# One attention and expert kernel: the last pair's sums, copies and divisions in another order, and the last batch's token bookkeeping made inside the first expert tile

## The chip, the cores and the metric

The kernel runs on one core of one Trainium2 chip. The metric is the time of one execution in microseconds (us) on the device; "before" is the kernel as it stood, "after" the changed one. A core has five engines that run their own instruction streams side by side and wait for each other by semaphores: PE (TensorE, matrix products), DVE (VectorE), ACT (ScalarE), POOL (GpSimd) and SP (SyncE, here only an issuer of transfers). ACT, SP and POOL each issue DMA transfers, which 16 DMA engines then carry out. PE's clock has two levels, 1.2 and 2.4 GHz; the profile lists what was granted in a stretch as a share of the upper one, so 0.50 is the lower level and 1.00 the upper.

## What is computed

Attention for 4 batches and 12 heads over 448 positions with heads of width 64, with a tanh cap on the scores. Its result, laid out as 1792 tokens of width 768, goes through a layer of 8 experts: each token goes to the one expert whose normalised embedding is nearest to it, and is scaled by a gate.

```python
scores = q @ k.T / sqrt(64)
scores = cap * np.tanh(scores / cap)
attn = softmax(scores)
x = (attn @ v)                      # as 1792 tokens x 768
logits = (x / |x|) @ (emb / |emb|).T / tau
expert = argmax(logits)             # one of 8
gate = softmax(logits)[expert]
out[expert == e] = gate * (relu(x @ w1[e]) @ w2[e])   # w1: 768x1024, w2: 1024x768
```

## The kernel before, in words

**Attention.** The 48 heads are worked as 24 pairs, six for each batch. The loop `for i in range(NPAIRS + 1)` in `attention_bounded` runs, in each pass, the scores of pair i (`scores`, four pieces u = 0 to 3) and the values of pair i-1 (`values`, also four pieces); the probabilities go to SBUF as `prob`. The sums over the keys that the softmax is divided by are not taken by a reduction but by adding blocks of `prob` (`add_keys`: one DVE addition at L792, two or three more at L798 and L800 on POOL, for the last pair half of them on DVE) and then multiplying by ones on PE (`norms`, tile `d`, L837, copied to `ds` by DVE at L839). `norms_t` transposes `ds` and takes reciprocals (`inv`). `rows` transposes the unnormalised output `xt` of a pair back to tokens (tile `xb`, L861) and divides it on DVE into `xsb` (L866). `router` and `router_t` make the experts' logits (`lp`, `ls`, `lt`, `lgh` at L897).

The order on every engine inside this function is the order in which the code is written (`tc.manual_schedule`). Work that follows a pair is put into a list of steps (`after`, `later`), and `do_later` takes the next step at fixed points of the loop; `fill` is a second list, of halves of the first expert's weights that are split into two 16-bit parts (`split_first`, ACT L221 and DVE L222).

**The first expert.** The tokens of batches 0 to 2 are known before the last batch, so the expert with the most of them is started early. After the loop its first tile of 128 tokens is transposed (`transpose_x`, PE L212; ACT casts it to `xh`, DVE takes the rest `xl` at L216), then 12 blocks of 12 matmuls (`up`, tile `hp`, PE L231) make the hidden layer in two halves. Between the blocks the loop `while later or ups` places one step of the last two pairs each: `norms`, `norms_t`, `router`, `router_t`, `rows` twice, `write_rows`. Then `tile0` runs the 8 down products of this tile (`down`, tile `yp`, PE L638). Its `hooks` place other work ahead of a down product: hook 12 holds `choose` (the last batch's choice of expert, DVE L414 to L422) and `all_norms` (squares on ACT L384, a power on POOL L387), hook 15 `count_last` (`rank` and `counts` on PE L443 to L458, then some 20 small DVE rows from L473 to L590), hook 16 `scales_x` and `gates` (DVE L397 to L427). Near its end the next tile is transposed, and DVE's L668 and ACT's L669 scale the result.

**The second tile.** `tile_body(0, idx0[:, 1:2], ...)` stands behind the branch that chose the attention arm. Its hook 0 holds `order` (the order of the other experts: `perm`, `which_e`, `pos_e`, DVE L1174 to L1183), `start_loads` (SP reads `pos_e` into registers and issues ten transfers of the next expert's weights, `w1r` and `w2r`, 6 MB in all), `gates_out` (four DVE rows, then ACT writes two columns of 448 token rows to DRAM, L407 and L410: 8 bytes for each token), and `slots` (DVE: `every`, `gn`, `first_t`; the one-hot rows `a_all` at L484; about 16 small rows from `both` to `slot`; the wide comparison `bm` at L1216). Hook 8 holds `fill_table`: PE's `tabp` (L1227) needs `bm` and `a_all`; DVE turns it into `table` (L1228), POOL copies a column to `idx_in` (L197) and gathers 128 token rows `xg` from DRAM (L198), which become `x_tile` of the third tile (L204). This gather reads what the gates' write has put into DRAM, so it waits for that write too.

The third tile and those after it split the next expert's weights on ACT and DVE while PE works.

## Time and profile before

| | |
|---|---|
| median of 3 runs | 546.03 us (545.84, 546.03, 549.48) |
| the profiled execution, its own time | 543.88 us |
| its span, first to last instruction | 542.1 us |
| mean granted clock of PE over the span | 0.963 |
| busy share: PE, DVE, ACT, POOL | 89%, 61%, 55%, 45% |

The change touches a stretch from about 225 to 282 us of the span. The busy shares are means over all stages and tell little of it; the rows below are from that stretch. Times in them count from the start of the span.

### The profile page before, as it was taken

How to read it: one execution, taken by the hardware profiler on the slowest of the kernel's cores; microseconds unless marked ns; L12 is line 12 of the kernel's file. 1: busy time of each engine (PE TensorE's matmuls, PEld its weight loads, DVE VectorE, ACT ScalarE, POOL GpSimd, SP SyncE). 2: the span in 40 equal slices, each digit the busy share in tenths (PEclk: the TensorE clock that was granted, in tenths of full speed). 3: DMA queues.
4: the chain of work that ended last, by engine and by line, in shares of the span. 5: the costliest groups of instructions: out<-in, count | busy, mean ns of one | idle time of the engine just before them, and what ended most of it. 6: DMA issues, size and time to landing. Idle time of an engine off the chain costs nothing. (4 is left out here: it accounts for less than half of the span.)

```text
span 542.1 us, 11950 instructions
## 1 busy us (share of the span) xinstructions
PE 482.8 (89%) x4603; PEld 312.3 (58%) x4604; DVE 329.5 (61%) x712; ACT 300.5 (55%) x371; POOL 245.6 (45%) x294
## 2 busy tenths in 40 slices
PE   3999999999997979979698799999999999998970
PEld 1444444444443434347676578877887788777650
DVE  4876686868698679588719521771125812496710
ACT  3987789788978887926128210831115511567410
POOL 2567556564643454640136412843235623553531
PEclk9999999999999979989999799999999999998995
DMA  7433218331451540325299711491112931297921
GB/s 228 128 112 113 76 63 289 111 112 67 148 207 62 190 160 0 104 73 164 97 390 365 282 40 59 175 344 59 61 60 96 382 114 61 87 366 258 332 86 39
DMA packets 30595, 83.51 MB, mean 154 GB/s; under 512 B 7293, under 2 KB 7449, under 8 KB 30498
## 3 DMA queue, kind: packets, MB, share of 16 engines
q1 hardware_dynamic: 26354, 67.68, 35.7%
q0 software_dynamic: 2896, 13.00, 6.8%
q10 hardware_dynamic: 1248, 1.64, 0.9%
q8 instruction: 47, 0.77, 0.6%
q14 instruction: 50, 0.41, 0.2%
HBM read 69.91 MB, written 13.00 MB: 153 GB/s over the span
## 5 line engine op out<-in xcount | busy, mean ns | idle before, releaser
L780 ACT ACTIVATE prob<-s,icap 128x896 f32<-128x896 f32 x96 | 86.3, 904 | 24.7 <-PE s L774 16.7
L794 POOL TENSOR_TENSOR sums<-sums,prob 128x896 f32<-128x896 f32 x23 | 48.4, 2102 | 81.8 <-DVE sums L792 62.7
L231 PEld LDWEIGHTS <-h 128*128 128x128 f16 x1056 | 79.7, 99 | 7.4 <-issue 3.8
L784 ACT ACTIVATE prob<-prob,cap_b 128x896 f32<-128x896 f32 (+1 forms) x64 | 81.7, 1277 | 2.1
L231 PE MATMUL h<-xh,h 128*128 128x128 f16 (+1 forms) x480 | 78.7, 218 | 2.6 <-ACT x_tile L669 1.4
L231 PE MATMUL h<-xl,h 128*128 128x128 f16 (+1 forms) x480 | 78.8, 218 | 0.9 <-issue 0.9
L231 PE MATMUL h<-xh,l 128*128 128x128 f16 (+1 forms) x480 | 78.8, 218 | 0.5 <-issue 0.4
L811 PE MATMUL v<-prob,vb 128*64 128x448 f32 x288 | 72.2, 581 | 2.9 <-DVE xt L826 2.8
L800 POOL TENSOR_TENSOR sums<-sums,prob 64x448 f32<-64x448 f32 x47 | 64.6, 1375 | 3.6
L204 POOL TENSOR_TENSOR x_tile<-xg 128x768 f32<-128x768 f32 x17 | 25.3, 1489 | 83.8 <-PE xt L212 74.1
L231 PEld LDWEIGHTS <-l 128*128 128x128 f16 x528 | 51.8, 99 | 1.1 <-issue 1.1
L215 ACT CAST xh<-xt 128x384 f16<-128x384 f32 x32 | 13.9, 481 | 68.5 <-PE xt L212 60.5
L244 DVE SCALAR_TENSOR_TENSOR hl<-h,hh 128x512 f16<-128x512 f32 (+1 forms) x20 | 13.3, 664 | 62.6 <-ACT hh L243 62.6
L243 ACT ACTIVATE hh<-h 128x512 f16<-128x512 f32 (+1 forms) x20 | 11.5, 574 | 67.1 <-PE h L231 67.1
L774 PE MATMUL s<-hi 64*128 64x448 f32 x144 | 35.5, 484 | 14.1 <-DVE hi L756 11.8
L1388 PE MATMUL h<-xh,h 128*128 128x160 f16 x192 | 41.1, 237 | 5.1 <-ACTq L1526 2.6
L216 DVE TENSOR_TENSOR xl<-xt,xh 128x384 f16<-128x384 f32 x32 | 16.4, 551 | 46.3 <-ACT xh L215 46.2
L638 PEld LDWEIGHTS <-hh 128*128 128x128 f16 (+1 forms) x352 | 32.9, 100 | 19.4 <-issue 1.2
L222 DVE SCALAR_TENSOR_TENSOR l<-w1r,by_pos,h 128x1024 f16<-128x1024 f32 x30 | 37.7, 1305 | 9.8 <-ACT h L221 9.8
L774 PEld LDWEIGHTS s<-hi 64*128 64x128 f32 x144 | 14.4, 190 | 46.9 <-ACT prob L780 16.0
L1388 PE MATMUL h<-xh,l 128*128 128x160 f16 x192 | 41.1, 238 | 0.0
L1388 PE MATMUL h<-xl,h 128*128 128x160 f16 x192 | 41.0, 237 | 0.0
(312 smaller groups left out, 1132.0 us busy)
## 6 DMA issues: line engine op xcount, KB each, us to landing
w1r<-in_moe_w_dram SPq DMA_DIRECT2D x36, 512.0 KB, 6.8
w2r<-in_moe_w_dram SPq DMA_DIRECT2D x24, 768.0 KB, 7.2
qkb<-in_qk_pairs_dram SPq DMA_DIRECT2D x11, 960.0 KB, 5.1
vb<-in_v_pairs_dram SPq DMA_DIRECT2D x12, 512.0 KB, 5.7
x_dram<-xsb SPq DMA_DIRECT2D x4, 1152.0 KB, 6.5
ring<-in_moe_w_dram SPq DMA_DIRECT2D x6, 512.0 KB, 3.9
ring<-in_moe_w_dram SPq DMA_DIRECT2D x8, 384.0 KB, 3.2
x_dram<-xsb ACTq DMA_DIRECT2D x1, 1152.0 KB
```

The source lines that it names most:

```text
L204: nc.gpsimd.tensor_tensor(x_tile, xg[:, :D], xg[:, SCALE : SCALE + 1].to_broadcast([P, D]), op=ALU.mult)
L216: nc.vector.tensor_tensor(lo, t, hi, op=ALU.subtract)
L222: nc.vector.scalar_tensor_tensor(out=lo, in0=raw, scalar=scale, in1=hi, op0=ALU.mult, op1=ALU.subtract, accum_out=acc)
L231: nc.tensor.matmul(hp[:, f, :W], l[j][:, c], x[:, j, :W], start=j == 0 and f == 0 and n == 0, stop=j == DC - 1 and f == 3 and n == 2, skip ...
L638: nc.tensor.matmul(y, hidden[h][l][:, c, o : o + k], w2p[p % 2][w][f // 2][:, f % 2, m * C : (m + 1) * C], start=f == 0 and n == 0, stop=f ...
L774: nc.tensor.matmul(sp[:, s, :S], l[sl, kc], r[sl, :], start=n == 0, stop=n == 2)
L780: nc.scalar.activation(o, d, AF.Tanh, scale=icap)
L784: nc.scalar.activation(o, o, AF.Exp, scale=cap_b)
L794: nc.gpsimd.tensor_tensor(t, t, pt[:, 4:6, :], op=ALU.add)
L800: eng.tensor_tensor(t[sl, s, :], t[sl, s, :], pt[sl, 6, :], op=ALU.add)
L811: nc.tensor.matmul(o[s * DH : (s + 1) * DH, :S], vb[:, u, s * DH : (s + 1) * DH], pt[:, 2 * u + s, :], start=u == 0, stop=False, skip_grou ...
L1388: nc.tensor.matmul(o, w1p[p % 2][l][j][:, c], x[:, j, :], start=j == 0 and f == fs[0] and m == 0, stop=j == DC - 1 and f == fs[-1] and m == 2,
```

## The change

Three things are done.

1. **The last pair's sums, copies and divisions.** `add_keys` is cut into `add_two`, `add_third` and `add_left`. For pair 23 `add_two` is placed in the loop ahead of the copy of pair 22's output; of the other additions, those of the second head stay on POOL, and those of the first are put one by one on DVE between the divisions `xsb`. The copy of pair 23's output (`xt`) and the copies `ds` of pairs 22 and 23 move from DVE to ACT.
2. **The choice and the counts.** `do_later` takes no step before the first up block, so the transposed tile's first block stands ahead of `norms`. `choose(b)` is placed behind `router_t`, ahead of the two `rows`; `count_last` behind them, ahead of `write_rows`.
3. **The slots and the experts' order.** `slots` is cut into `slots_1`, `token_rows`, `slots_2` and `fill_masks`. In `tile0`, hook 12 now holds `all_norms`, hook 14 `slots_1`, hook 15 `scales_x` and `gates`, hook 16 `slots_2` and `order`. Hook 0 of the second tile keeps `start_loads`, `token_rows`, `fill_masks` and `gates_out`, in this order.

```diff
-        def tile0(todo, space):
+        def tile0(todo, space, counted=False):
...
-            hooks[12] += [lambda: choose(last), lambda: all_norms(last)]
-            hooks[15] += [count_last]
-            hooks[16] += [lambda: scales_x(last), lambda: gates(last)]
+            if counted:
+                hooks[12].insert(0, lambda: all_norms(last))
+                hooks[14] += [lambda: slots_1()]
+                hooks[15] += [lambda: scales_x(last), lambda: gates(last)]
+                hooks[16] += [lambda: slots_2(), order]
...
+            def add_two(i):
+                pt = prob[i]
+                t = sums[i] = apool.tile([P, 2, S], F32, tag="sums", name=f"sums{i}", bufs=3)
+                nc.vector.tensor_tensor(t, pt[:, 0:2, :], pt[:, 2:4, :], op=ALU.add)
+
+            def add_third(i, s, eng):
+                eng.tensor_tensor(sums[i][:, s, :], sums[i][:, s, :], prob[i][:, 4 + s, :], op=ALU.add)
+
+            def add_left(i, s, eng):
+                sl = slice(s * DH, (s + 1) * DH)
+                eng.tensor_tensor(sums[i][sl, s, :], sums[i][sl, s, :], prob[i][sl, 6, :], op=ALU.add)
+
             def add_keys(i):
-                pt = prob[i]
-                t = apool.tile([P, 2, S], F32, tag="sums", name=f"sums{i}", bufs=3)
-                nc.vector.tensor_tensor(t, pt[:, 0:2, :], pt[:, 2:4, :], op=ALU.add)
-                if i < NPAIRS - 1:
-                    nc.gpsimd.tensor_tensor(t, t, pt[:, 4:6, :], op=ALU.add)
+                if i == NPAIRS - 1:
+
+                    add_third(i, 1, nc.gpsimd)
+                    add_left(i, 1, nc.gpsimd)
+                    return
+                add_two(i)
+                nc.gpsimd.tensor_tensor(sums[i], sums[i], prob[i][:, 4:6, :], op=ALU.add)
                 for s in range(2):
...
-                    nc.vector.tensor_copy(x, o[:, :S])
+                    (nc.vector.tensor_copy if i < NPAIRS - 1 else nc.scalar.copy)(x, o[:, :S])
...
-                nc.vector.tensor_copy(ds, d[:, :S])
+                (nc.vector.tensor_copy if i < NPAIRS - 2 else nc.scalar.copy)(ds, d[:, :S])
...
+                if j == NPAIRS - 1:
+                    steps.insert(4, lambda: choose(b))
+                    steps += [nop, count_last]
...
+                        if i == NPAIRS and u < 2:
+                            (add_third, add_left)[u](j, 0, nc.vector)
...
+                        if (i, u) == (NPAIRS - 1, 2):
+                            add_two(i)
...
                 while later or ups:
-                    do_later()
+                    if len(ups) < 2 * DC:
+                        do_later()
...
     hooks1 = {
-        0: [order, start_loads, lambda: gates_out(last), slots],
+        0: [start_loads, lambda: token_rows(last), fill_masks, lambda: gates_out(last)],
```

Three places show how the instructions move. In the rows, `l` is the low part of a split weight, `ring` its raw piece, `hl` the low part of the hidden layer; numbers behind names tell buffers apart.

DVE around the last pair's sums, before:

```order
L826 COPY xt_2193<-v_2135 128x448
L897 TENSOR_TENSOR lgh<-lt_2195,inv_2000 128x3x64
L897 TENSOR_TENSOR lgh<-lt_2195,inv_2000 64x64
L222 SCALAR_TENSOR_TENSOR l_154,sums<-ring_178,first_s,h_150 128x384
L792 TENSOR_TENSOR sums_2205<-prob_2125 128x896
L798 TENSOR_TENSOR sums_2205<-sums_2205,prob_2125 128x448
L800 TENSOR_TENSOR sums_2205<-sums_2205,prob_2125 64x448
L866 TENSOR_TENSOR xsb<-xb_2214,inv_2000 128x3x128
```

And DVE at the same place after:

```order
L845 TENSOR_TENSOR sums_2190<-prob_2129 128x896
L888 COPY xt_2199<-v_2139 128x448
L959 TENSOR_TENSOR lgh<-lt_2201,inv_2004 128x3x64
L959 TENSOR_TENSOR lgh<-lt_2201,inv_2004 64x64
L222 SCALAR_TENSOR_TENSOR l_154,sums<-ring_178,first_s,h_150 128x384
L848 TENSOR_TENSOR sums_2190<-sums_2190,prob_2129 128x448
L928 TENSOR_TENSOR xsb<-xb_2217,inv_2004 128x3x128
L928 TENSOR_TENSOR xsb<-xb_2217,inv_2004 64x128
L222 SCALAR_TENSOR_TENSOR l_154,sums<-ring_179,first_s,h_150 128x384
L852 TENSOR_TENSOR sums_2190<-sums_2190,prob_2129 64x448
L928 TENSOR_TENSOR xsb<-xb_2229,inv_2004 128x3x128
```

Three additions in a row ahead of the first division have become one ahead of the copy, one ahead of the first division and one ahead of the second.

DVE between the last division and the last batch's choice, before:

```order
L866 TENSOR_TENSOR xsb<-xb_2365,inv_2000 128x3x128
L866 TENSOR_TENSOR xsb<-xb_2365,inv_2000 64x128
L244 SCALAR_TENSOR_TENSOR hl_210,acc_213<-hp_2257,hh_209 128x512
L222 SCALAR_TENSOR_TENSOR l_156,sums<-ring_180,first_s,h_152 128x384 x2
L222 SCALAR_TENSOR_TENSOR l_157,sums<-ring_178,first_s,h_153 128x384 x2
L222 SCALAR_TENSOR_TENSOR l_157,sums<-ring_179,first_s,h_153 128x384 x2
L244 SCALAR_TENSOR_TENSOR hl_212,acc_213<-hp_2258,hh_211 128x512
L414 TENSOR_REDUCE lg<-lgh 128x32
```

And DVE from the end of the choice to the counts, after:

```order
L420 TENSOR_REDUCE fm_2367<-first_2364 128x4
L422 TENSOR_TENSOR oh_all<-iota_v,fm_2367 128x32
L244 SCALAR_TENSOR_TENSOR hl_214,acc_217<-hp_2261,hh_213 128x512
L222 SCALAR_TENSOR_TENSOR l_156,sums<-ring_180,first_s,h_152 128x384
L928 TENSOR_TENSOR xsb<-xb_2386,inv_2004 128x3x128
L928 TENSOR_TENSOR xsb<-xb_2386,inv_2004 64x128
L222 SCALAR_TENSOR_TENSOR l_156,sums<-ring_180,first_s,h_152 128x384
L928 TENSOR_TENSOR xsb<-xb_2407,inv_2004 128x3x128
L928 TENSOR_TENSOR xsb<-xb_2407,inv_2004 64x128
L222 SCALAR_TENSOR_TENSOR l_157,sums<-ring_178,first_s,h_153 128x384 x2
L473 TENSOR_TENSOR own_2454<-rp_2442,oh_all 128x32
```

The choice now stands ahead of the two divisions `xsb`, and the counts (from L473) follow them behind two split steps. PE's rank product L443 takes the PSUM buffer that the first of these two divisions reads, and L457 the buffer of the second (there are two, `ps_t`).

DVE at the start of the second tile, before:

```order
L1174 TENSOR_TENSOR perm<-iota_t,place 128x64
L1181 TENSOR_TENSOR which_e<-perm,iota_t 1x64
L1183 TENSOR_REDUCE pos_e<-which_e 1x8
L432 TENSOR_REDUCE gs_4029<-ex 128x4
L433 TENSOR_SCALAR gs_4029<-gs_4029 128x4
L434 RECIPROCAL gs_4029<-gs_4029 128x4
L435 TENSOR_TENSOR xsb<-gs_4029,p2x 128x4
L1187 TENSOR_TENSOR every<-done_full,halves 128x8
```

And after:

```order
L484 TENSOR_SCALAR a_all<-iota_p,rowf,tok 128x128 x4
L1242 TENSOR_TENSOR bm<-iota_t,slot 128x640
L432 TENSOR_REDUCE gs_4095<-ex 128x4
L433 TENSOR_SCALAR gs_4095<-gs_4095 128x4
L434 RECIPROCAL gs_4095<-gs_4095 128x4
L435 TENSOR_TENSOR xsb<-gs_4095,p2x 128x4
```

The order of the experts has gone to the first tile, and the four rows of the gates, which ACT's write waits for, stand behind `a_all` and `bm` now.

## Rows read from the trace of the kernel before

**Rows 1.** Timeline of PE: start, duration, engine, line, what; in brackets the wait ahead.

```profile
234.20 0.52 PE L212 MATMUL xt<-ident,x_tile 128*128 128x128 f32 x3 [2.72 <-DVE xsb L866]
...
236.41 1.72 PE L837 MATMUL d<-sums,ones 128*32 128x448 f32 x8
238.07 0.29 PE L231 MATMUL hp<-xh,h 128*128 128x128 f16 x1
...
243.56 0.22 PE L231 MATMUL hp<-xh,h 128*128 128x128 f16 x1
...
244.23 0.50 PE L861 MATMUL xb<-ident,xt 128*128 128x128 f32 x3
...
249.36 0.49 PE L638 MATMUL yp<-h,hh 128*128 128x384 f16 x2
...
260.32 0.22 PE L231 MATMUL h<-xh,h 128*128 128x128 f16 x1 [1.38 <-ACT x_tile L669]
...
268.50 0.56 PE L1227 MATMUL tabp<-bm,a_all 128*128 128x40 f16 x16 [2.66 <-DVE bm L1216]
...
279.92 0.88 PE L212 MATMUL xt<-ident,x_tile 128*128 128x128 f32 x6 [0.38 <-POOL x_tile L204]
```

**Rows 2.** Windows: length, busy PE, PEld, DVE, ACT, POOL; PE clock; DMA share, GB/s.

```profile
236.00:239.00 3.00, 3.00 (x20) 1.22 (x19) 2.72 (x7) 1.50 (x3) 2.22 (x4) 0.50 0.43 131
...
269.80:273.20 3.40, 2.95 (x30) 2.76 (x28) 0.97 (x3) 0.00 (x0) 1.06 (x1) 0.50 0.94 331
```

**Rows 3.** Timeline of DVE, same columns.

```profile
228.43 2.02 DVE L792 TENSOR_TENSOR sums<-prob 128x896 f32<-128x896 f32 x1
...
243.28 0.60 DVE L222 SCALAR_TENSOR_TENSOR l<-ring,first_s,h 128x384 f16<-128x384 f32 x1
...
243.81 0.74 DVE L866 TENSOR_TENSOR xsb<-xb,inv 128x384 f32<-128x384 f32 x2
...
250.98 0.85 DVE L414 TENSOR_REDUCE lg<-lgh 128x32 f32<-128x384 f32 x1
...
253.40 0.19 DVE L473 TENSOR_TENSOR own<-rp,oh_all 128x32 f32<-128x32 f32 x1 [0.46 <-PE cp L458]
...
256.04 0.16 DVE L397 COPY p2x<-den 128x4 f32<-128x4 f32 x1
...
257.87 1.02 DVE L216 TENSOR_TENSOR xl<-xt,xh 128x384 f16<-128x384 f32 x2 [0.66 <-ACT xh L215]
...
261.88 0.23 DVE L1174 TENSOR_TENSOR perm<-iota_t,place 128x64 f32<-128x64 f32 x1 [2.22 <-issue]
...
263.80 0.97 DVE L484 TENSOR_SCALAR a_all<-iota_p,rowf,tok 128x128 f16<-128x128 f16 x4
264.69 0.16 DVE L1196 SCALAR_TENSOR_TENSOR both<-done_full,tails 128x8 f32<-128x8 f32 x1
...
267.62 0.82 DVE L1216 TENSOR_TENSOR bm<-iota_t,slot 128x640 f16<-128x640 f32 x1
```

**Rows 4.** Timeline of ACT (ACTq: a transfer that it issues).

```profile
263.33 0.56 ACTq L407 DMA_DIRECT2D x_dram<-xsb  x1
```

**Rows 5.** Timeline of POOL.

```profile
253.96 1.05 POOL L387 TENSOR_TENSOR den<-den,half_b 128x4 f32<-128x4 f32 x1 [15.17 <-ACT junk L384]
...
270.46 1.06 POOL L198 DMA_INDIRECT xg<-x_dram,idx_in  x1 [0.90 <-DMA w1r<-in_moe_w_dram]
```

**Rows 6.** Timeline of SP, the next expert's first weights.

```profile
267.45 3.37 SPq L1155 DMA_DIRECT2D w1r<-in_moe_w_dram  x6
```

**Rows 7.** The line L410 between 255 and 270 us, issue to landing of its transfer.

```profile
DMA to landing us min/median/max: 2.9/2.9/2.9
```

**Rows 8.** DMA queues, 264.2 to 265.8 us: packets, MB, share of 16 engines' time.

```profile
q10 hardware_dynamic: 480, 0.00, 16.2%
```

**Rows 9.** DMA queues, 269.5 to 274.5 us, the weights.

```profile
q1 hardware_dynamic: 483, 1.76, 97.2%
```

**Rows 10.** DMA queues, 2 to 4.5 us: 4-byte packets beside the first loads.

```profile
q10 hardware_dynamic: 145, 0.00, 3.0%
```

More of the change, by code (lines that the diff above doesn't have):

```diff
@@ L496, in attention_moe @@
         idx0 = small.tile([P, 2], I32, tag="idx0", name="idx0")
+        slot = small.tile([P, G], F32, tag="slot", name="slot")
+        first_t = small.tile([P, E], F32, tag="first_t", name="first_t")
+        pos_e = small.tile([1, E], I32, tag="pos_e", name="pos_e")
+        perm = small.tile([P, E, E], F32, tag="perm", name="perm")
         def first_expert(cp):
@@ L724, in count_last, with order @@
             tiles(c[:, :E])
-        def tile0(todo, space):
+        def order():
+            nc.vector.tensor_tensor(
+                perm,
+                iota_t[:, :E].unsqueeze(2).to_broadcast([P, E, E]),
+                place.unsqueeze(1).to_broadcast([P, E, E]),
+                op=ALU.is_equal,
+            )
+            which = small.tile([1, E, E], F32, tag="which_e", name="which_e")
+            nc.vector.tensor_tensor(which, perm[0:1], iota_t[0:1, :E].unsqueeze(1).to_broadcast([1, E, E]), op=ALU.mult)
+            with nc.allow_low_precision("numbers of experts, exact"):
+                nc.vector.tensor_reduce(pos_e, which, axis=AX.X, op=ALU.add)
@@ L734, in tile0 @@
             hooks = {2 * DC + f: [lambda n=2 * (5 - f): split_until(n)] for f in range(6)}
-            hooks[12] += [lambda: choose(last), lambda: all_norms(last)]
-            hooks[15] += [count_last]
-            hooks[16] += [lambda: scales_x(last), lambda: gates(last)]
+            if counted:
[3 more added lines that the diff above has]
+                hooks[16] += [lambda: slots_2(), order]
+            else:
+                hooks[12] += [lambda: choose(last), lambda: all_norms(last)]
+                hooks[15] += [count_last]
+                hooks[16] += [lambda: scales_x(last), lambda: gates(last), slots_1, slots_2, order]
             tile_body(0, idx0[:, 0:1], None, hooks=hooks, hidden=first_h, space=space)
@@ L1009, in attention_bounded @@
                 yp = ps_s.tile([P, 2, 512], F32, tag="s", name="yp")
-                tile0(fill, (lambda n, i: yp[:, i, :384] if n == "y" else x_tile, (ps_t, "tt")))
+                tile0(fill, (lambda n, i: yp[:, i, :384] if n == "y" else x_tile, (ps_t, "tt")), True)
         def attention_any():
@@ L1146, in attention_moe @@
     pos_i = work.tile([1, 2, E], I32, name="pos_i")
-    pos_e = work.tile([1, E], I32, name="pos_e")
-    perm = work.tile([P, E, E], F32, name="perm")
     table = work.tile([P, NTAB], I32, name="table")
@@ L1170, in split2 @@
         load2(p + 1, f)
-    def order():
-        nc.vector.tensor_tensor(
-            perm,
-            iota_t[:, :E].unsqueeze(2).to_broadcast([P, E, E]),
-            place.unsqueeze(1).to_broadcast([P, E, E]),
-            op=ALU.is_equal,
-        )
-        which = work.tile([1, E, E], F32, tag="which_e", name="which_e")
-        nc.vector.tensor_tensor(which, perm[0:1], iota_t[0:1, :E].unsqueeze(1).to_broadcast([1, E, E]), op=ALU.mult)
-        with nc.allow_low_precision("numbers of experts, exact"):
-            nc.vector.tensor_reduce(pos_e, which, axis=AX.X, op=ALU.add)
@@ L1215, in slots, with fill_masks @@
+    def fill_masks():
         bm = work.tile([P, G, NTAB], F16, tag="bm", name="bm")
@@ L1221, in slots @@
         )
-        cp.update(b=bm, t=first_t)
+        cp.update(b=bm)
     def fill_table(start):
@@ L1240, in positions @@
         )
-        nc.vector.tensor_tensor(val[:, 4, :], cp["t"], done, op=ALU.add)
+        nc.vector.tensor_tensor(val[:, 4, :], first_t, done, op=ALU.add)
         pv = work.tile([P, NV, E, E], F32, tag="pv", name="pv")
```

63 lines of the change are left out of this document (28 added, 35 removed).

## The prediction, made before the changed kernel was run

> **What bounds the kernel now.** I read the page for where PE idles, then the timelines of PE and DVE between 225 and 282 us, and last the queues that the second tile's gather hangs on. In this stretch PE has three gaps, and DVE's work stands behind each of them. The first is 2.72 us ahead of the first tile's transposes, which wait for a division `xsb` to free their buffer [rows 1]; the division stands behind L792, which took 2.02 us, and two more additions [rows 3]. The second is 1.38 us ahead of the second tile, for L669 [rows 1]. The third is 2.66 us ahead of `tabp`, which waits for `bm` [rows 1]. Two stretches at the lower clock belong to these gaps: 236.0 to 239.0 us and 269.8 to 273.2 us had a granted clock of 0.50, the 1.2 GHz level, each a little after PE came back from a gap of over 2.6 us [rows 1, 2]. All later work of this expert follows from the second tile's end, so a shift there goes through to the end of the kernel. I name two instants: Y, the first down product (249.36 before), and T, the second tile's first matmul (260.32 before), 10.96 us later [rows 1].
>
> **The change part by part.** *Ahead of Y.* The first addition now stands ahead of a copy that DVE had to wait for anyway, and of the other two one stands ahead of each of the two divisions that hold up the transposes. So the first division comes some 3.4 us earlier (L792's 2.02 and an addition of about 1.4, an estimate from it for the smaller tile beside POOL), and the first transposes come right behind the last values, at 231.5 (234.20 less the wait of 2.72) [rows 1, 3]. The second division has only L792's 2.0 us less ahead of it, and holds the second half up as before. The product `d` stood between the transposes and the first block for 1.66 us (236.41 to 238.07) [rows 1] and now comes behind that block; the cast and `xl` of the second half, which it covered, take some 0.7 of this. The hidden layer therefore starts 3.0 earlier, near 235.1. The 12 blocks and their steps took 11.29 us up to Y, the first 0.93 at the lower clock [rows 1, 2], so 10.8 at the upper. To that come `d` at about half its duration, 0.9, the nine narrow rank and count products, 0.25 (an estimate), and a new wait: PE's rank product needs the buffers that the two divisions read, and DVE has put the choice ahead of them. The choice takes 1.96 us (250.98 to 252.94, where the next row began to wait) [rows 3]. Behind the last logits DVE has that, three split steps of 0.53 (243.28 to 243.81), the hidden layer's low half, which I take as a split step, and two divisions at 0.74: 5.6, behind some 0.8 for the logits themselves. PE has five blocks at 0.67 (243.56 to 244.23) and two sets of transposes at 0.50 [rows 1, 3], 4.3. So PE stands for 2.1 us. Y without a clock loss is 235.1 + 10.8 + 0.9 + 0.25 + 2.1 = 249.2, as before. But between the values and the first block PE still has 3.6 us with little more than the transposes in it (231.5 to 235.1), so about 2.9 of gaps; before, a gap of 2.72 there brought 3 us at the lower clock [rows 1, 2]. I take such a stretch again, now wholly among blocks, at +1.6. Ends: 0 and, if the 2.1 us wait brings a fall of its own, 3.2. So Y is at 250.9.
>
> *From Y to T.* The copies that go to ACT cost nothing: ACT was busy for 1.50 of 3.00 us there [rows 2]; if that cover failed, each would add about a split step's 0.53. The counts, 2.64 us (253.40 to 256.04) [rows 3], end at about Y + 0.7 and with the last splits, the low half and `slots_1` DVE is done by Y + 3.1, under the wait for the norms. This wait is new as a bound: the four squares and POOL's power ended 255.01, Y + 5.65 [rows 5], and depend on ACT alone. Behind it DVE has `scales_x` and `gates`, 1.16 to the last row's end; `slots_2`, 2.93 (264.69 to 267.62) [rows 3]; `order`, three of the seven rows between 261.88 and the gates' write at 263.33 [rows 3, 4], so about 0.65; and only then `xl`, which before waited for nothing but its cast. From `xl` to T it took 2.45 (257.87 to 260.32) [rows 1, 3]. The sum is 5.65 + 1.16 + 2.93 + 0.65 + 2.45 = 12.85 against 10.96: T comes 1.9 later after Y. PE's part ended 1.38 us ahead of T before, at Y + 9.6 [rows 1]; without the rank products among it I put it at Y + 8.8, so PE idles some 4 us ahead of the second tile. With Y, T moves by +1.9 + 1.6 = **+3.5**.
>
> *From T to the third tile.* DVE comes back from the branch at T + 1.56 (261.88) [rows 3]. It has `a_all`, 0.89 (263.80 to 264.69), and `bm`, 0.74 net, so `bm` is there at T + 3.2, while PE reaches `tabp` at T + 5.5 (268.50 less the wait of 2.66): that wait goes, and with the steps from `tabp` to the gather unchanged, 1.96 (268.50 to 270.46) [rows 1, 5], the table alone would let the gather go at T + 7.5, against T + 10.14 before. The gather also waits for the gates' write. Its DVE rows, 0.8, now stand behind `bm`, so ACT issues it at T + 4.0 instead of T + 3.0 [rows 4]. And the weights go first: they were issued 5.57 us after `order` began (267.45 less 261.88) [rows 3, 6], `order` now begins 3.1 us ahead of T, and so the 6 MB of weights start at T + 2.5 instead of T + 7.1. Before, the write had the engines to itself: its 448 small packets, 28 on each of 16 engines, lay in 1.6 us at 16.2% of the engines' time [rows 8], and it landed 2.9 us after its second half, some 3.5 after its first [rows 4, 7]. Behind weights each small packet may have to wait for a large one. The trace shows no write of this kind among them, so I bound it. Below, no wait at all: 3.5. Next, one 4 KB packet each, 0.97 x 5.0 x 16 / 483 = 0.161 us [rows 9]: 28 x 0.161 = 4.5, and 2.3 that is not traffic (3.5 less about 1.2 of packets within the 1.6 us), 6.9. Above, as for the 4-byte packets beside the first loads, 2.5 x 16 / 145 = 0.276 us each [rows 10]: 7.7 and 2.3, 10.0. I take 6.9, since rows 9 are the same transfers on the same queue, and rows 10 show that small packets do wait for large ones, one by one. The gather then starts at T + 4.0 + 6.9 + 0.3 = T + 11.2, **+1.1** (ends -2.3, where PE's own work ends the gain, and +4.2). Who waits: POOL's gather, behind it `x_tile`, then PE's transposes at 279.92, which waited 0.38 us for it before [rows 1].
>
> PE has by then been idle: without the wait for `bm` it comes to those transposes at T + 16.5 (19.6 less 2.66 and 0.38), or 1.7 earlier if the clock holds, and `x_tile` comes at T + 20.7, so over 4 us of gap, and with it a lower clock as at 269.8, 1.3 us after the return at 268.50 [rows 1, 2]. Behind the gap come the transposes and two of the eight down products, 2.7 by the 8.8 us of the first tile; 1.3 at the upper clock and the rest doubled makes **+1.2** (ends 0 and 1.4). In the third tile DVE and ACT carry the bound with their splits, so nothing more is lost there, and nothing is given back.
>
> The sum is 3.5 + 1.1 + 1.2 = +5.8 on the profiled execution, 543.88, so 549.7; the median of the runs lies 2.15 above that execution, and on it the forecast is 546.03 + 5.8 = **551.8 us**. A measurement of this kernel tells about 1%, 5.5 us, from no change: 540.6 and 551.5 are the bounds.
>
> **The rivals.** *The gates' write slips through.* If several of its small packets go for each large one, it lands about as it did, the gather starts near T + 7.8, and PE, not the gather, decides the second tile: some 2.2 us less there. Against +3.5 at T that leaves +1.3, **547.3**, not slower than one can measure (545.5 to 548.5). It decides from a mean wait under about 0.12 us for each packet, where the gather comes as early as before. For it: the packets were cheap before, 16.2% over 1.6 us [rows 8]; against it: in rows 10 a small packet took 0.276 us of an engine's time, more than the 0.161 of a large one in rows 9. The Trainium skill, "DMA: Bandwidth & Descriptors", section "Queues, rings and completion order", says that a DMA engine goes round its queues a whole packet at a time, of some 9 to 17 descriptors. By that rule 28 elements would wait for two or three turns, and this rival would hold; rows 10 do not agree with it, and it gets one in five.
>
> *The gaps shrink and the clock stays.* If the first division comes early enough that PE's clock doesn't fall, and PE's rank product finds its buffers free (if PE is late itself), Y comes 2.1 us earlier; with the write slipping through, T moves by -0.2 and the rest by -2.2: -2.4, **543.6** (542.5 to 545.5). For it: the gap ahead of the first transposes does shrink. Against it: DVE's 5.6 us are durations without any wait among them, so they have nothing to lose.
>
> *The falls add up.* If the 2.1 us wait brings a clock fall of its own (+1.6) and the write takes 10.0 us, the sum is 5.1 + 4.2 + 1.2 = +10.5, **556.5** (555 to 558).
>
> **How the numbers follow.** The forecast's case, 549 to 555, gets 0.50; the write that slips through 0.20; the faster case 0.13; the falls that add up 0.12; 0.05 is left for what I don't see. The range takes in the forecast's case, the slower edge of the faster one and all of the first rival: 544.5 to 555.5. Faster by over 1% needs more than any case here gives: 0.04. Within 1% lie the first rival, most of the second and the lower part of the forecast's case, 0.46; slower 0.50.
>
> **What would show it.** After the change, PE should wait some 2 us at the rank product for DVE's division (L928), and there should be a gap of about 4 us ahead of the second tile, ended by L673 and DVE's row ahead of it. `tabp` should wait for nothing. SP's first `w1r` should be issued ahead of ACT's L407, whose landing should take 7 us or more instead of 2.9, and POOL's gather should be released by that. The windows should show the lower clock early in the hidden layer and again around the transposes of the third tile's tokens. The prediction is wrong if the landing stays near 3 us, if T lies less than 1 us later than before, or if the end of the kernel doesn't follow the second tile's end.

## The result, and the profile after

The changed kernel took 554.06 us (median of 7 runs, 552.0 to 558.44) against 546.03 before (7 runs, 545.13 to 549.48): 1.0142 times as long, 95% interval 1.0109 to 1.0174. Here and below, a ratio leaves out single runs over 1.5% longer than the fastest of their kernel, so it can differ a little from the ratio of the medians. The profiled execution took 558.16, span 556.5 us, so it is one of the longer ones; that of the kernel before (543.88, span 542.1) was shorter than all of its seven runs. The spans of the two traces therefore lie 14.4 us apart, the medians 8.0. With Y for the first down product and T for the second tile's first matmul, as in the prediction, and X for the transposes of the tokens that the second tile's gather brings:

| us | before | after |
|---|---|---|
| last values' end (the wait ahead of the first transposes taken off) | 231.48 | 233.87 |
| from there to Y | 17.88 | 22.50 |
| Y to T | 10.96 | 12.52 |
| T to the gather's issue | 10.14 | 15.88 |
| T to X | 19.60 | 24.42 |
| X to the end of the span | 262.2 | 263.2 |

The first row is no effect of the change that can be told: in a second trace of code that is the kernel before up to Y (e3 below) the last values ended at 234.73.

The timeline of PE after, from the first transposes to X, answers to [rows 1]:

```profile
234.45 0.52 PE L212 MATMUL xt<-ident,x_tile 128*128 128x128 f32 x3 [0.58 <-DVE xsb L928]
237.32 0.88 PE L212 MATMUL xt<-ident,x_tile 128*128 128x128 f32 x3 [2.35 <-DVE xsb L928]
...
240.24 1.72 PE L899 MATMUL d<-sums,ones 128*32 128x448 f32 x8
...
251.91 0.19 PE L443 MATMUL rp<-oh_all,upper 128*128 128x32 f16 x1 [0.79 <-DVE xsb L928]
...
253.12 0.26 PE L457 MATMUL cp<-oh_all,ones 128*128 128x8 f16 x4 [0.91 <-DVE xsb L928]
...
256.37 0.85 PE L642 MATMUL yp<-h,hh 128*128 128x384 f16 x2
...
268.89 0.26 PE L231 MATMUL h<-xh,h 128*128 128x128 f16 x1 [3.37 <-ACT x_tile L673]
...
276.91 0.56 PE L1253 MATMUL tabp<-bm,a_all 128*128 128x40 f16 x16
...
293.31 1.54 PE L212 MATMUL xt<-ident,x_tile 128*128 128x128 f32 x6 [6.22 <-POOL x_tile L204]
```

The first wait has shrunk from 2.72 to 0.58, but the second half of the transposes now waits 2.35. The wait for `bm` ahead of `tabp` is gone. In its place stand 0.79 and 0.91 at the rank and count products, 3.37 ahead of T, and the largest of all, 6.22 ahead of X. What stands behind that one is in the timelines of ACT, SP and POOL after [rows 4, 5, 6]:

```profile
272.46 0.56 ACTq L407 DMA_DIRECT2D x_dram<-xsb  x1
...
271.25 3.35 SPq L1223 DMA_DIRECT2D w1r<-in_moe_w_dram  x6
...
277.77 0.21 POOL L197 COPY idx_in<-table 128x1 int32 x1 [6.38 <-DVE table L1254]
284.77 1.06 POOL L198 DMA_INDIRECT xg<-x_dram,idx_in  x1 [6.78 <-DMA w2r<-in_moe_w_dram]
```

The gather had its table at 278.0 and was issued 6.78 us later. The profile puts this wait down to a load of weights. The gather reads no weights; it has to wait for both parts of the gates' write, whose last packets went between 283 and 283.5. POOL's semaphore instructions for the gather began at 283.7, so I count 11.2 us from ACT's issue to the landing. That it is this write which holds the gather, e1 and e10 show below. The queues say why it is late. Here are two windows of the DMA queues after, 273.5 to 277 us and then 277 to 280.5 us (packets, MB, share):

```profile
q1 hardware_dynamic: 307, 1.12, 98.6%
...
q10 hardware_dynamic: 18, 0.00, 0.3%
...
q1 hardware_dynamic: 376, 1.37, 97.1%
q10 hardware_dynamic: 348, 0.00, 5.7%
```

The first weights were issued 1.2 us ahead of the write. In the first window hardly any of the write's packets (q10) go; in the second they go nearly one for one with the weights' packets (q1, most of them of 4 KB); the last 114 follow in the 3 us after it. Before, all 480 went within 1.6 us [rows 8].

The lower clock shows in five windows after (columns as in [rows 2]):

```profile
238.50:240.00 1.50, 1.02 (x10) 1.01 (x10) 1.50 (x3) 0.73 (x2) 1.50 (x2) 0.50 0.65 164
240.00:243.00 3.00, 3.00 (x22) 1.35 (x21) 0.20 (x2) 0.89 (x2) 0.51 (x3) 0.50 0.57 178
...
252.00:256.00 4.00, 3.09 (x43) 2.99 (x44) 3.90 (x24) 0.61 (x1) 0.00 (x0) 0.75 0.46 177
256.00:257.50 1.50, 1.50 (x10) 0.98 (x8) 1.43 (x8) 0.88 (x2) 0.00 (x0) 0.52 1.06 369
...
294.50:298.00 3.50, 3.50 (x13) 1.74 (x12) 1.11 (x2) 0.70 (x2) 2.09 (x6) 0.50 0.56 134
```

There is one stretch of some 6 us from the second transposes into the first blocks, a second behind the waits at the rank products, up to the first down products, and one behind the 6.22 us gap.

DVE after shows the collisions with POOL and the new tail of the first tile [rows 3]:

```profile
230.27 1.90 DVE L222 SCALAR_TENSOR_TENSOR l<-ring,first_s,h 128x384 f16<-128x384 f32 x1 [0.97 <-ACT h L221]
...
232.10 1.54 DVE L848 TENSOR_TENSOR sums<-sums,prob 128x448 f32<-128x448 f32 x1
...
262.10 0.17 DVE L397 COPY p2x<-den 128x4 f32<-128x4 f32 x1 [3.07 <-POOL den L387]
...
263.19 0.16 DVE L754 SCALAR_TENSOR_TENSOR both<-done_full,tails 128x8 f32<-128x8 f32 x1
...
266.64 1.00 DVE L216 TENSOR_TENSOR xl<-xt,xh 128x384 f16<-128x384 f32 x2
```

DVE stands 3.07 us for the norms and then does 3.45 us of slots and order (263.19 to 266.64) ahead of `xl`.

### The profile page after: what moved, and what is told of

It is laid out like the page before. It is cut to its first block, busy times and chain, and to the rows that moved or that the text cites. A ratio compares the mean times of both kernels' runs of the same rounds, so it can differ in the third digit from the quotient of the medians.

```text
span 556.5 us, 11951 instructions
## 1 busy us (share of the span) xinstructions
PE 489.7 (88%) x4603; PEld 317.6 (57%) x4604; DVE 330.2 (59%) x710; ACT 301.8 (54%) x373; POOL 244.8 (44%) x294
## 5 line engine op out<-in xcount | busy, mean ns | idle before, releaser
L231 PEld LDWEIGHTS <-h 128*128 128x128 f16 x1056 | 81.8, 101 | 11.6 <-issue 6.2
L231 PE MATMUL h<-xh,h 128*128 128x128 f16 (+1 forms) x480 | 80.1, 220 | 5.0 <-ACT x_tile L673 3.4
L231 PE MATMUL h<-xh,l 128*128 128x128 f16 (+1 forms) x480 | 80.1, 220 | 1.9 <-issue 1.9
L231 PE MATMUL h<-xl,h 128*128 128x128 f16 (+1 forms) x480 | 80.1, 220 | 0.1
L852 POOL TENSOR_TENSOR sums<-sums,prob 64x448 f32<-64x448 f32 x47 | 63.4, 1348 | 3.6
L243 ACT ACTIVATE hh<-h 128x512 f16<-128x512 f32 (+1 forms) x20 | 11.5, 574 | 66.6 <-PE h L231 66.6
L827 PEld LDWEIGHTS s<-hi 64*128 64x128 f32 x144 | 14.4, 190 | 48.9 <-ACT prob L833 17.5
L642 PE MATMUL y<-h,hl 128*128 128x384 f16 (+1 forms) x160 | 39.2, 336 | 2.4 <-DVE hl L244 2.4
```

The costliest lines, as they stand in the source:

```text
L231: nc.tensor.matmul(hp[:, f, :W], l[j][:, c], x[:, j, :W], start=j == 0 and f == 0 and n == 0, stop=j == DC - 1 and f == 3 and n == 2, skip ...
L642: nc.tensor.matmul(y, hidden[h][l][:, c, o : o + k], w2p[p % 2][w][f // 2][:, f % 2, m * C : (m + 1) * C], start=f == 0 and n == 0, stop=f ...
L827: nc.tensor.matmul(sp[:, s, :S], l[sl, kc], r[sl, :], start=n == 0, stop=n == 2)
L852: eng.tensor_tensor(sums[i][sl, s, :], sums[i][sl, s, :], prob[i][sl, 6, :], op=ALU.add)
```

## The experiments

Theory A: the loss is the gates' write, which now meets the weights, and ahead of it the second tile's later start, by slots and order that stand between the norms and `xl`. Theory B: the loss is the front, the wait at the rank products and the falls of the clock, and the gather's delay is hidden. Each ratio is the kernel's time over that of the kernel before, run beside it on the same chip. e0 to e3 ran on one chip, e4 to e7 on a second and e8 to e11 on a third, so between these groups ratios are compared and not medians.

| run | median, us | ratio (95% interval) | Y to T | write issued, T + | gather, T + | T to X |
|---|---|---|---|---|---|---|
| e0_after_again | 555.28 | 1.0150 (1.0108 to 1.0191) | 12.51 | 3.50 | 15.53 | 24.09 |
| e1_gates_first | 546.41 | 0.9998 (0.9977 to 1.0018) | 12.47 | 1.31 | 10.10 | 18.37 |
| e2_gates_in_tile0 | 549.07 | 1.0029 (1.0002 to 1.0055) | 12.51 | 0.09 | 8.83 | 17.47 |
| e3_before_gates_last | 558.87 | 1.0210 (1.0177 to 1.0242) | 10.96 | 8.17 | 19.14 | 28.09 |
| e4_sums_as_before | 548.58 | 1.0009 (0.9983 to 1.0035) | 12.51 | 1.48 | 9.92 | 18.02 |
| e5_slots_under_norms | 544.05 | 0.9911 (0.9880 to 0.9943) | 10.68 | 0.09 | 8.12 | 16.79 |
| e6_counts_later | 546.82 | 0.9982 (0.9948 to 1.0016) | 13.59 | 1.31 | 8.95 | 17.24 |
| e7_all_three | 550.09 | 1.0034 (1.0010 to 1.0058) | 13.42 | 0.09 | 12.43 | 21.01 |
| e8_order_behind_gates | 545.62 | 0.9959 (0.9933 to 0.9985) | 10.35 | 0.09 | 7.30 | 16.36 |
| e9_parts_1_2_only | 546.27 | 0.9971 (0.9941 to 1.0000) | 10.53 | 3.03 | 10.30 | 19.62 |
| e10_weights_held_back | 546.11 | 0.9961 (0.9932 to 0.9990) | 11.89 | 3.09 | 8.55 | 17.33 |
| e11_adds_behind_xl | 543.03 | 0.9891 (0.9854 to 0.9928) | 11.65 | 0.09 | 7.39 | 17.34 |

The last four columns are from the one profiled execution of each. They repeat well wherever the order of the instructions is the same. What varies from one execution to the next is the stretch ahead of Y, called the front below, and in it the length of the first fall of the clock.

**e0_after_again**: the changed kernel once more.

> The changed kernel itself once more, as the base of the runs beside it and for a second trace. Both theories: 552 to 556 us, 6 to 9 over before. In the trace the gates' write should again take 9 to 12 us from issue to landing among the weights' packets, PE should again wait 1.5 to 2.5 us in all at the rank and count products, and the second tile should begin 12 to 13 us after the first down product. What is open is how many stretches at the lower clock there are: the first trace had one in the first blocks and a second ahead of the first down product; if the second is chance, this trace may lack it and be some 2 us shorter.

555.28 us, 1.015. The second trace is like the first: 0.79 and 0.91 at the rank products, both stretches at the lower clock, 22.65 from the last values to Y. The second fall is no chance of one trace; of the eight traces with this order up to Y (after, e0, e1, e2, e5, e8, e9, e10) only e1's lacks it, though PE waits 0.79 and 0.91 there too. So the waits alone don't settle it.

**e1_gates_first** and **e2_gates_in_tile0**: the write ahead of the weights, in two ways.

```diff
-        0: [start_loads, lambda: token_rows(last), fill_masks, lambda: gates_out(last)],
+        0: [lambda: gates_out(last), start_loads, lambda: token_rows(last), fill_masks],     # e1
+        0: [start_loads, lambda: token_rows(last), fill_masks],                              # e2, and
             tile_body(0, idx0[:, 0:1], None, hooks=hooks, hidden=first_h, space=space)
             nc.vector.tensor_tensor(sum_h[:, :2], sum_h[:, :2], acc0, op=ALU.add)
+            gates_out(last)
```

> The gates' four DVE rows stand at the head of the second tile again, ahead of the token rows and the mask; nothing else differs from the changed kernel. Theory A (most of the loss is the gates' write behind the weights): ACT issues the write about 1.6 us earlier, at T + 2.0 to 2.4, together with the first weights, so it meets far fewer of them: landing 4 to 8 us after the issue instead of 11, gather at T + 8 to 11 instead of T + 16, and 4 to 6 us less than the changed kernel, 548 to 550. Rival B (the loss is the later start of the second tile and the clock; the gather's delay is hidden): within 1 us of the changed kernel, 552 to 555.

> The gates' four DVE rows and the write are made at the end of the first tile, behind its last scaling on DVE and ahead of the branch; nothing else differs from the changed kernel. Theory A: the write is issued near T + 0.5, two us ahead of the first weights, lands after 3 to 5 us, and the gather is held by the table alone, at T + 8 to 10; 5 to 7 us less than the changed kernel, 547 to 549. What is left over before (1 to 3 us) is the later start of the second tile. Rival B: within 1 us of the changed kernel, 552 to 555, since the second tile starts no earlier.

By their ratios both are 1.2 to 1.5% shorter than the changed kernel: B falls. In e1 four small rows moved by two places take back the whole loss, 8.9 us of medians, more than A had expected. These are ACT's issue and the gather of e1:

```profile
267.48 0.56 ACTq L407 DMA_DIRECT2D x_dram<-xsb  x1
...
276.27 1.06 POOL L198 DMA_INDIRECT xg<-x_dram,idx_in  x1 [0.90 <-DMA w1r<-in_moe_w_dram]
```

The gather comes when its table does. e2 has the still earlier write and the shorter way from T to X, and yet a median 2.7 us over that of e1, at the edge of their intervals; its trace has the two falls ahead of Y, e1's has none. e1's traced execution had DVE's first addition at 3.48 us beside POOL's, the last values late and hardly a gap behind them. What decides that between two kernels whose code is the same to the end of the first tile was not found, nor whether it is what the medians differ by.

**e3_before_gates_last**: the kernel before with this one thing alone.

```diff
-        0: [order, start_loads, lambda: gates_out(last), slots],
+        0: [order, start_loads, slots, lambda: gates_out(last)],
```

> The kernel before, with one thing of the change alone: the gates' rows and write stand behind the slots and the mask in the second tile's hook, so the weights are issued ahead of them; the first tile is as it was. Theory A: the write is issued near T + 8.5 to 9, 1.5 us after the first weights, lands some 10 us later, the gather starts near T + 19 to 20 instead of T + 10.1, PE waits for the tokens for 8 to 10 us, and the time is 8 to 11 us over before, 554 to 557. Rival B: the gather's delay costs nothing, 545 to 548.

2.1% longer than before, 12 us, more than the 8 to 11 that A had expected. The write's issue, the gather and the transposes in the trace of e3:

```profile
273.05 0.56 ACTq L407 DMA_DIRECT2D x_dram<-xsb  x1
...
284.02 1.06 POOL L198 DMA_INDIRECT xg<-x_dram,idx_in  x1 [7.64 <-DMA w2r<-in_moe_w_dram]
...
292.97 1.54 PE L212 MATMUL xt<-ident,x_tile 128*128 128x128 f32 x6 [5.88 <-POOL x_tile L204]
```

Here no instruction of the front or of the first tile differs from before. The write is also issued 5.2 us later than before (T + 8.17 for 3.01), but at the 3.5 us that it took there it would have landed at T + 11.7, about when the gather had its table (276.38, T + 11.5); the 7.64 us of wait are the weights'.

**e10_weights_held_back**: the changed kernel with the write as late as it was, and the weights behind it.

```diff
-                hooks[16] += [lambda: slots_2(), order]
+                hooks[16] += [lambda: slots_2()]
...
-        0: [start_loads, lambda: token_rows(last), fill_masks, lambda: gates_out(last)],
+        0: [lambda: token_rows(last), fill_masks, lambda: gates_out(last), order, start_loads],
```

> The changed kernel with the order of the experts moved behind the gates' rows in the second tile's head; the gates' write is issued as late as in the changed kernel (T + 3.6), but SP learns the order only behind it and the weights start near T + 9. Theory A (the write is slow because weights are ahead of it, not because it is issued late): landing 3 to 4 us after the issue, gather near T + 7.5 to 8, PE's wait of 6 us ahead of the tokens goes, 545 to 548, some 8 us less than the changed kernel. Rival G (the write is late since its rows stand behind the mask): 551 to 555.

546.11, 0.996 of before. In the trace of e10 the write was issued at T + 3.09, within half a microsecond of the changed kernel's, its second part took

```profile
DMA to landing us min/median/max: 3.1/3.1/3.1
```

and the gather was held by its table. So it is not the late issue, it is the weights ahead of it. Rival G falls.

**e4_sums_as_before** and **e9_parts_1_2_only**: what the other parts are worth. e4 is e1 with the sums and copies of the last pair as they were before; e9 has the first two parts of the change and, from the slots on, the old order:

```diff
-                hooks[14] += [lambda: slots_1()]
-                hooks[15] += [lambda: scales_x(last), lambda: gates(last)]
-                hooks[16] += [lambda: slots_2(), order]
+                hooks[16] += [lambda: scales_x(last), lambda: gates(last)]
...
-        0: [start_loads, lambda: token_rows(last), fill_masks, lambda: gates_out(last)],
+        0: [order, start_loads, lambda: gates_out(last), slots_1, lambda: token_rows(last), slots_2, fill_masks],
```

> The kernel with the gates' rows first in the second tile (546.4 before), and with the first part of the change taken back: the last pair's additions stand together on DVE behind its pair, and the copies of the last output and of the sums are on DVE. Theory A (the new order of the sums brings the hidden layer forward by some 2.4 us as the traces showed, and nothing later hides that): 1 to 3 us longer than the same kernel with the new order, 547.5 to 549.5. Rival C (the additions wait for POOL's either way and the gain is lost at the rank products and in the clock): 545.5 to 547.

> The change without its third part: the sums, copies, choice and counts as in the changed kernel, but the slots, the order of the experts and the gates' write in the second tile, in the order they had before. The write is ahead of the weights as it was. Theory A: the second tile begins at Y + 9.5 to 10.5 (no slots ahead of it), and from there all is as before, so 544 to 547, at or a little under before; the whole loss belongs to part three. Rival B (the loss is the front: the wait at the rank products and the falls of the clock): 549 to 553.

e4 is within 0.1% of e1: the new order of the sums is worth nothing that can be measured (the intervals leave room for 0.6%). e9 is 0.3% under before, its interval reaching to 1: the first two parts gain a little at most, and the third carries the loss.

**e5_slots_under_norms** and **e8_order_behind_gates**: e5 is e2 with the slots in DVE's wait for the norms; e8 has the experts' order behind the gates' rows as well.

```diff
-                hooks[14] += [lambda: slots_1()]
+                hooks[14] += [lambda: slots_1(), lambda: slots_2(), order]     # e5; e8: no order here
                 hooks[15] += [lambda: scales_x(last), lambda: gates(last)]
-                hooks[16] += [lambda: slots_2(), order]
...
             gates_out(last)
+            order()                                                            # e8
```

> The kernel with the gates' write at the end of the first tile (549.1), and with the slots and the order of the experts ahead of the scales on DVE, where DVE stood for 3.1 us for the norms, instead of behind them. Theory A (the second tile comes late because 3.6 us of slots and order stand between the norms and xl): the second tile begins at Y + 9.5 to 10 instead of Y + 12.5, and the time falls by 2 to 3 us, to 546 to 547; a little of that may go back, since the order of the experts, and with it the weights, come earlier by 3 us and meet the gates' write. Rival D (the second tile's start is hidden by the wait for the tokens): within 1 us of 549.

> The kernel with the slots under the wait for the norms and the gates' write at the end of the first tile (544.05, 0.991 of before), with one more move: the order of the experts stands behind the gates' rows there, so SP learns it some 4 us later and the weights start near T + 5 instead of T + 0.1. Theory A: the gates' write no longer meets weights (landing 3 to 4 us after its issue instead of 7), 0.65 us of DVE's path ahead of xl goes, the wait of 1.25 us for the tokens goes: 541.5 to 543.5. Rival F (the weights are needed early: the third tile's splits wait for them): 545 to 548.

e5 is 0.9% under before and 1.2% under e2, a little better than A had expected, with T at Y + 10.68 instead of 12.51, though the weights came back to meet the write (both issued at T + 0.1; it took some 7 us). So in the trace the slots' place costs the 1.9 that the prediction had said. From Y to X the two traces differ by 2.5 us, 0.5%; where the rest of the 1.2% comes from is not shown. e8 missed: its trace is shorter in each column of the table but the write's issue, which is the same, and its ratio 0.5% above that of e5, the intervals just overlapping. F, that the third tile needs the weights early, stays open: from X to the end of the span e8 took 261.7, e5 260.5, but e11 260.2 with weights as late as in e8 (T + 5.7).

**e6_counts_later**: e1 with the counts behind the rows' write and one empty step.

```diff
-                    steps += [nop, count_last]
+                    steps += [nop]
                 if j % NP == NP - 1:
                     steps.append(lambda: write_rows(b, 0, D))
+                if j == NPAIRS - 1:
+                    steps += [nop, count_last]
```

> The kernel with the gates' rows first (546.4), and with the last batch's counts one and a third blocks later: the write of the rows and one empty step stand ahead of them. Theory A (PE stands 1.7 us for the divisions at the rank and count products): that wait shrinks to 0.3 to 0.6, Y comes 1.2 us earlier, and since DVE ends its counts no later the second tile too: 544.5 to 546. Rival E: the norms' chain on ACT starts with the same second relu, so the gain of Y goes through in full or, if DVE's counts come later and hold the slots up, not at all: 546 to 547.5.

PE's wait went from 1.70 to 0.54, and Y to T grew by 1.1: DVE's counts moved into the first tile's own work. 0.998 against 1.000, no difference that can be told, as rival E had it.

**e7_all_three** and **e11_adds_behind_xl**: two ways to take the additions out of the way of the divisions. In e7 PE adds the last blocks of the last pair itself (four more products into `d`), with the counts of e6 and the slots of e5; e11 is e8 with DVE's two additions behind `xl` and the steps one block later.

```diff
+                    if more:                                                                             # e7
+                        sl = slice(s * DH, (s + 1) * DH)
+                        nc.tensor.matmul(o, ones32, prob[k][:, 4 + s, :], start=False, stop=False, skip_group_check=True)
+                        nc.tensor.matmul(o, ones32[sl], prob[k][sl, 6, :], start=False, stop=True, skip_group_check=True)
...
-                        if i == NPAIRS and u < 2:                                                        # e11
-                            (add_third, add_left)[u](j, 0, nc.vector)
...
                 scale_x()
+                add_third(NPAIRS - 1, 0, nc.vector)
+                add_left(NPAIRS - 1, 0, nc.vector)
...
-                    if len(ups) < 2 * DC:
+                    if len(ups) < 2 * DC - 1:
```

> The version that the runs point to: the gates' write at the end of the first tile, slots and order under the wait for the norms, the counts later, and for the last pair the second and third additions are no longer made on DVE and POOL, but taken by PE as four more products into the tile of the sums (the result is the same sum). Theory A: no addition stands ahead of the divisions, so the first blocks start some 2 us earlier again and PE's gap ahead of them is under 1.5 us; the lower clock at the first blocks goes away with it (up to 1.6 us); with the second tile at Y + 10: 540.5 to 543.5, faster than both kernels. Rivals: the gap stays because the second half waits for the cast and xl anyway, 543.5 to 546; or the weights, now earlier, meet the gates' write and give back 2 us or more, 545 to 547.

> The version with the order behind the gates, and with DVE's two additions of the last pair behind xl instead of between the divisions, the first step of the last pairs one block later. Theory A (the divisions wait for the additions, each 1.5 us beside POOL's): the divisions come 2 to 3 us earlier, PE's wait of 2.4 us ahead of the second half of the transposes goes, the clock more often holds in the first blocks, and with 1 to 2 us less to Y: 540 to 542.5. Rival C (the front's gain is lost at the rank products, which hang on DVE's chain behind the last sums): no change against the run beside it, within 1 us.

e7 is a miss, longer than before. In both the transposes come without a wait, as meant, but in e7 the products into the tile of the sums cost far more than before (timeline of PE, e7):

```profile
241.16 1.32 PE L898 MATMUL d<-sums,ones 128*32 128x448 f32 x6
242.27 1.70 PE L901 MATMUL d<-prob,ones 128*32 128x448 f32 x2
243.90 1.48 PE L902 MATMUL d<-prob,ones 64*32 64x448 f32 x2
245.31 0.94 PE L898 MATMUL d<-sums,ones 128*32 128x448 f32 x2
246.08 0.91 PE L901 MATMUL d<-prob,ones 128*32 128x448 f32 x2
```

The tile took 6.7 us instead of 1.7, at a granted clock of 0.75. Twice as many products at the 1.72 for eight that they took at the lower clock before [rows 1] would be 3.4; the other half stays open. Nor does it look like `prob` as such: the two products over `sums` at 245.31 took 0.77 to the next start, those over `prob` behind them 0.85. Besides, this execution was 5.7 us over the median of e7, and had a stall of 5.72 of which the last section tells. e11 is the best version, 1.1% under before and some 0.7% under e8, just short of what A had expected, and as in e7 its divisions don't stand behind an addition. Its front is shorter, 18.8 us from the transposes' start to Y against 20.9 in e8, with no fall of the clock among the first blocks. But its second fall lies behind Y, Y to X is 2.3 longer than in e8, and X to the end 1.5 shorter. So the traces don't show which stretch the 0.7% comes from.

## Why the prediction was right, and where its sizes were not

The time, 554.06, lies inside the range, on the side that was forecast, 2.3 us over the predicted 551.8. That the gates' write, now behind the weights, holds up the gather is shown: e1, e2 and e10 take the weights out of the write's way and the loss goes; e3 puts them in its way in the kernel before and brings it.

*Y to T.* Forecast 12.85, measured 12.52, in every trace with that order. The wait for the norms, the slots behind it and PE's gap (3.37 for "some 4") are as worked out, and e5 shows what the slots' place costs: 1.83 of the trace.

*T to the gather.* The write was issued at T + 3.57 (forecast 4.0), the weights at T + 2.36 (2.5). The landing was forecast at 6.9 with an upper end of 10.0, and was 11.2: this is the term that was mis-sized. The price of one packet was right: 3.5 x 16 / 348 is 0.161 us of an engine for a small packet and the large one beside it, the figure that the forecast took from [rows 9], so 28 of them take 4.5. Wrong was the "2.3 that is not traffic": among the weights the packets began to go 3.5 to 4 us after the issue, not 1.2 as before, and the last 114 came between 280.5 and 283.5. Why they begin so late was not measured. The upper end rested on a wrong reading: in [rows 10] the small packets took 3.0% of the engines' time, 0.008 us each; the 0.276 is how far apart they came, not what one took. So +1.1 for the gather's start became +5.7, of which the gather's own landing (6.9 instead of 7.8 us, since most weights had passed) and the time that PE had to spare gave a little back: T to X is 4.8 longer.

*Ahead of Y.* Forecast +1.6 with ends 0 and 3.2; measured from the last values +4.6 in one trace and +4.8 in the other. Part of that is chance. The first fall of the clock was some 3 us long before and 6 in both of these traces, but e3, with the front of before, also has 6 and takes 19.2 us from the last values to Y, and e8, e9 and e10, with the front of the change, have 3 and take 20.8 to 20.9. Like against like the front is 2.9 to 3.5 us longer in the traces. Two terms failed. PE's wait at the rank products was right (1.70 for 2.1), but behind it stands the second fall of the clock, which was in the rival where the falls add up and not in the forecast; e6 and e7, with only 0.54 of that wait, don't have it, e1, with all of it, neither. And the divisions came less early than "some 3.4 us" and "2.0" (2.1 and 0.7 against the last values): the additions that were taken apart still met POOL's, 1.54 us each, and a split between them took 1.90 where [rows 3] has 0.60, so the second half of the transposes waits 2.35. The step that costed the first addition at nothing, because it stands ahead of a copy that waits anyway, holds in most traces (1.08 us). It failed in two, e1 and e7, where it waited 3.4 us beside POOL's work and PE waited 2.4 to 2.5 us for the copy behind it (timeline of DVE, e1):

```profile
227.91 3.48 DVE L845 TENSOR_TENSOR sums<-prob 128x896 f32<-128x896 f32 x1
```

With e4 this suggests why part one is worth nothing: it moves a collision instead of taking it away. e11 does take it away from the divisions.

*Behind X.* The lower clock is there as forecast (1.54 for the transposes, 0.50 behind them), and X to the end grew by 1.0 for the 1.2 forecast.

*The sum.* What repeats in both traces of the changed kernel, from Y on, is +6.8 and +7.4 us of the 8.0 by which the medians differ, where the forecast had 1.9, 1.1 and 1.2. The forecast is some 3 us short there, all of it between T and X. The front has about 1 us left on the medians, less than the 1.6 forecast, though the traces have it at about 3 or more; e9, with the new front, is even 0.3% under before. The mechanism was right, but that the time lies inside the range is in part luck: with the +4.6 of the trace it would have been near 558.

Of the rivals, the write does not slip through: in both traces of the changed kernel the packets go nearly one for one (348 to 376, and 374 to 410 in e0). The Trainium skill, "DMA: Bandwidth & Descriptors", section "Queues, rings and completion order", has the engine drain a packet of some 9 to 17 descriptors before it turns to the next queue; if that were what is counted here, small packets would far outnumber the large ones in the second window, and 348 to 376 does not agree. One for one is no fixed rule either: in e5, where write and weights were issued together, the window from 268.2 to 270.2 us has

```profile
q1 hardware_dynamic: 141, 0.51, 77.3%
q10 hardware_dynamic: 400, 0.00, 11.2%
```

The clock did not stay up, and of the case in which the falls add up (556.5) the traces have both halves, two falls ahead of Y and a landing over 10 us; the median lies between it and the forecast.

## What to carry to other kernels

Moving work forward also moves the transfers that it triggers: ask of each small write that something waits for which bulk load it will now stand behind, and issue it first, or hold the load back. A row that waits for another engine is a place for work that doesn't: slots moved from behind the wait for the norms to under it brought the second tile 1.83 us nearer. Taking apart a run of additions gained nothing that could be measured here, where each piece still met the other engine's; look at the durations beside it, not at the count.

## What the runs showed of the hardware that was not expected

The 8-byte packets of a write issued 1.0 to 1.2 us behind a bulk load began to go only some 4 us after their issue (after, e0, e3); without a load it was 1.2 (before). From then on about as many of them went as of the load's in after and e0, but not always: in e3 204 of them went beside 95 of the load's in the first us, and in e5, with both issued together, 400 beside 141 in two.

Behind the branch DVE stood for 1.1 to 3.0 us in all traces without anything that the profile shows it to wait for; a second time for about 1 us in e1, e4 and e6, and in e7, whose weights were issued 0.5 us behind T, a second time for 5.72 us in the middle of four equal rows (timeline of DVE, e7):

```profile
275.18 0.32 DVE L484 TENSOR_SCALAR a_all<-iota_p,rowf,tok 128x128 f16<-128x128 f16 x1 [2.70 <-issue]
281.22 0.76 DVE L484 TENSOR_SCALAR a_all<-iota_p,rowf,tok 128x128 f16<-128x128 f16 x3 [5.72 <-issue]
```

The instruction queue (q14) had 5 packets between 272.5 and 282 us, among 593 of weights. Whether the fetch of code waited there is not shown; in e5, with weights issued as early, DVE stood only once, for 2.70.
